# The fp16 remainder of the squared activation: VectorE or GpSimd

## Chip, cores and metric

The kernel runs on one core of a Trainium2 chip. The core has five engines with queues of their own: TensorE (PE in the profile, with PEld for its weight loads), VectorE (DVE), ScalarE (ACT), GpSimd (POOL) and SyncE (SP), which issues the DMAs here. Each engine takes its instructions in the program's order and waits for the others by semaphores. The metric is the device time of one execution in microseconds.

## What is computed

The reference is a block-causal attention over 8 batches, 8 heads, 576 positions and a head size of 64, whose output is the input of a two-layer network with a squared ReLU. Everything is fp32.

```python
scores = scale * np.matmul(q, k.transpose(0, 1, 3, 2))
scores = np.where(block_i >= block_j, scores, -1000000000.0)   # blocks of 64
attn = np.exp(scores - np.max(scores, axis=-1, keepdims=True))
attn = attn / (np.sum(attn, axis=-1, keepdims=True) + 1e-09)
attn_out = np.matmul(attn, v)
...
x = attn_out.transpose(0, 2, 1, 3).reshape(4608, 512)
h = x @ w_in            # 512 x 2048
r = np.maximum(h, 0.0)
g = r * r
return g @ w_out        # 2048 x 512
```

## The kernel before

TensorE multiplies fp16 faster than fp32, so each fp32 operand is split into an fp16 number and an fp16 remainder. A product of two such operands is the sum of three fp16 matmuls: high times high, high times remainder, remainder times high. The inputs, the probabilities (`p_rows`), the normalized attention output (`xt`), both weights (`w1h`, `w1l`, `w2h`, `w2l`) and `g` are all kept as such pairs.

The 4608 tokens are worked on in 12 chunks of 384 (`CH`), numbered `ck` 0 to 11; the hidden size of 2048 is 16 tiles of 128, numbered `f`. For each chunk, `moe_in` makes the 16 hidden tiles and `moe_out` the three output tiles:

- L670: 12 matmuls make `ph` (128 x 384) of one `f` in PSUM. There are two such banks (pool `ps_m`), which `po` of `moe_out` shares.
- L676: ScalarE writes `r` = relu(`ph`) to SBUF, in a ring of three buffers.
- L678: ScalarE writes `g[:, 0]`, the square of `r` rounded to fp16.
- L679: GpSimd writes `r*r` in fp32 over `r`.
- L680: `g[:, 1]` = `r*r` - `g[:, 0]`, the fp16 remainder. GpSimd does this for `f` below 8 (`G_POOL`) of chunk 0 (`G_CK` is 1), VectorE for the other 184 of the 192 tiles. The `r` buffer is free after it.
- L695: 48 matmuls make each output tile `po` from the 16 pairs `g`; for each `f` the remainder is read by the third matmul, after the two that read `g[:, 0]`.
- L702: VectorE scales `po` into `ob`, and a DMA writes it out.

The attention runs beside this. A pass covers one pair of heads of one batch: `scores` on TensorE (L411 for fp32 operands, L422 for fp16 pairs), maxima on VectorE (L446, L449), exp on ScalarE (L452), sums and reciprocals on VectorE (L460, L461), the pair `p_rows` on ScalarE (L475) and VectorE (L476), a transposing DMA into `p_turned` (L480), and the product with v on TensorE (L534), which ScalarE writes to `x` (L541). `front` prepares the next pass: maxima of the loaded `qk` and `v` (L363, L364), scales by way of TensorE (L177 to L191) and the fp16 pairs of q, k and v (L382 to L400). `load` brings the operands of the pass after that.

When the four head pairs of a batch are done for a group of rows, `normalize` works out their norms (L579 to L595), and GpSimd multiplies `x` by them (L604), VectorE rounds to fp16 (L605), and GpSimd makes the remainder (L606). A batch has two such groups, so there are 16. The result is what `moe_in` reads.

In the first 250 us the weights are split as well (`weight_scale`, `weight_parts`, L245 to L292), with integer work on VectorE and the remainders `w1l` and `w2l` on GpSimd (L292).

The order of all this comes from two places. `fill`, with the tables `FILL` and `DELAY`, lays the steps of the chunks between the passes as the program is written; then the framework's scheduler orders the instructions of each engine by its own model of their durations (`schedule_with_timeline_sim=TLS`). An engine that is given to an instruction can so change the order of others.

Of the kernel before, what the change touches and what calls it, by code (L numbers as in the profile page):

```python
# [14 lines left out]
ALU = mybir.AluOpType  # L15
# [26 lines left out]
SCN = 1  # L42
PTN = 3
PT0 = 16
G_POOL = 8
G_CK = 1
X_POOL = 1
QF = (6, 7)
WT = 1
# [51 lines left out]
def attention_moe_kernel(ctx: ExitStack, tc: tile.TileContext, qkt, qk, vm, vt, w_in, w_out, out):  # L101
    nc = tc.nc
# [524 lines left out]
    def moe(ck):  # L627
        gs = yield from moe_in(ck)
        yield from moe_out(ck, gs)

    def first_moe(ck, firsts):

        scale, parts = weight_scale(1), weight_parts(1)
        hidden = moe_in(ck)
        n = 0
        while True:
            try:
                next(hidden)
            except StopIteration as e:
                gs = e.value  # L640
                break
            if n == IVN:
                for r in firsts:
                    inverses(*r)
            yield
            if next(parts0, 0) is None:
                yield
            for _ in range(SCN if n >= SC0 else 0):
                if next(scale, 0) is None:
                    yield  # L650
            if n == PT0:
                yield from scale
            for _ in range(PTN if n >= PT0 else 0):
                if next(parts, 0) is None:
                    yield
            n += 1
        for gen in (scale, parts):
            yield from gen
        yield from moe_out(ck, gs)

    def moe_in(ck):
        xt = xts.pop(ck)
        gs = []
        c = 2.0 ** (1 - A_X - A_W)
        for f in range(NF):
            ph = ps_m.tile([P, 512], F32, tag="mm", name=f"ph_{ck}_{f}")
            i = 0
            for cc in range(NHP):
                for w, z in ((w1h, 0), (w1h, 1), (w1l, 0)):
                    nc.tensor.matmul(  # L670
                        ph[:, :CH], w[:, f, P * cc : P * cc + P], xt[:, z, cc, :], start=(i == 0), stop=(i == 11)
                    )
                    i += 1
            r = p2.tile([P, 512], F32, tag="r", name=f"r_{ck}_{f}", bufs=3)
            r = r[:, :CH]
            nc.scalar.activation(r, ph[:, :CH], AF.Relu, scale=c)  # L676
            g = pg.tile([P, 2, CH], F16, tag="g", name=f"g_{ck}_{f}")
            nc.scalar.activation(g[:, 0], r, AF.Square)  # L678
            nc.gpsimd.tensor_tensor(r, r, r, op=ALU.mult)  # L679
            (nc.gpsimd if f < G_POOL and ck < G_CK else nc.vector).tensor_tensor(g[:, 1], r, g[:, 0], op=ALU.subtract)  # L680
            gs.append(g)
            yield
        return gs
# [204 lines left out]
```

## Time and profile before

| what | value |
|---|---|
| three runs, us | 1150.38, 1157.13, 1152.78 |
| median, us | 1152.78 |
| the profiled execution's own time, us | 1157.18 |
| its span in the profile, us | 1155.4 |
| mean granted TensorE clock | 0.963 |
| instructions | 18711 |

The span runs from the first instruction of the profile to the last; 1.8 us lie around it. In the profile's rows `out<-in` names the tiles written and read, L680 is line 680 of the kernel, and an arrow `<-` behind a wait names the instruction that ended it. A matmul's duration is its time in the pipeline, so successive matmuls overlap.

### The profile page before, as it was taken

Reading aid. Unit: us, or ns where it says so; the run is one execution under the profiler, and the core shown is the slowest. Engines: PE = TensorE matmul, PEld = TensorE weight load, DVE = VectorE, ACT = ScalarE, POOL = GpSimd, SP = SyncE. Lnnn points to the kernel's source line nnn. Section 1 sums busy time; section 2 is a strip of 40 time slices with the busy share of each in tenths; the row PEclk is TensorE's granted clock in tenths of the full one; section 3 lists DMA queues with packets and bytes.
Section 4 is the critical chain, followed back from the end, with each engine's and each line's share of the span. In section 5 each row is a group of like instructions: output and inputs, shape, how many; then the busy total and the mean of one; then the engine's idle time right before and its main releaser. Section 6 shows DMA issues by size and latency. Waiting matters only on the chain. (4 is left out here: it accounts for less than half of the span.)

```text
span 1155.4 us, 18711 instructions
## 1 busy us (share of the span) xinstructions
PE 1035.3 (90%) x6836; PEld 541.6 (47%) x6836; DVE 763.9 (66%) x1783; ACT 629.6 (54%) x1492; POOL 341.0 (30%) x312
## 2 busy tenths in 40 slices
PE   6679777898989989899997999889889999999998
PEld 4234322354445445445544545445445545555453
DVE  6998789869778978868749857976896613212120
ACT  6586765557468548726737627726865723223140
POOL 2575145124112412422205302520340314312030
PEclk9799998899999999999999999989999999999999
DMA  8555177867687688855954657567848330000000
GB/s 282 194 186 194 56 193 188 198 140 140 144 165 156 114 191 164 155 115 114 186 120 84 141 111 138 119 140 148 170 80 169 48 78 20 10 19 1 28 1 28
DMA packets 337948, 142.25 MB, mean 123 GB/s; under 512 B 309696, under 2 KB 323008, under 8 KB 337856
## 3 DMA queue, kind: packets, MB, share of 16 engines
q1 hardware_dynamic: 337856, 141.06, 55.2%
q8 instruction: 53, 0.87, 0.3%
q14 instruction: 39, 0.32, 0.1%
HBM read 55.31 MB, written 9.44 MB: 56 GB/s over the span
## 5 line engine op out<-in xcount | busy, mean ns | idle before, releaser
L670 PE MATMUL ph<-xt,w1h 128*128 128x384 f16 x1536 | 381.2, 330 | 21.7 <-ACT r L676 10.4
L695 PE MATMUL po<-w2h,g 128*128 128x512 f16 x1152 | 359.7, 386 | 8.5 <-ACT w2h L291 8.5
L679 POOL TENSOR_TENSOR r<-r 128x384 f32<-128x384 f32 x192 | 178.6, 936 | 556.4 <-ACT g L678 520.3
L695 PEld LDWEIGHTS <-g 128*128 128x128 f16 x1728 | 166.3, 99 | 219.4 <-issue 34.1
L670 PE MATMUL ph<-xt,w1l 128*128 128x384 f16 x768 | 253.3, 330 | 0.0
L695 PE MATMUL po<-w2l,g 128*128 128x512 f16 x576 | 222.1, 386 | 4.2 <-POOL w2l L292 4.2
L670 PEld LDWEIGHTS <-w1h 128*128 128x128 f16 x1536 | 145.0, 99 | 129.6 <-issue 34.4
L452 ACT ACTIVATE p<-ps,nmx,es 128x320 f32<-128x320 f32 (+8 forms) x216 | 131.1, 616 | 135.9 <-DVE nmx L449 111.4
L676 ACT ACTIVATE r<-ph 128x384 f32<-128x384 f32 x192 | 93.2, 491 | 160.3 <-PE ph L670 147.9
L680 DVE TENSOR_TENSOR g<-r,g 128x384 f16<-128x384 f32 x184 | 113.7, 623 | 86.3 <-POOL r L679 86.2
L476 DVE SCALAR_TENSOR_TENSOR p_rows<-p,rs,p_rows 128x320 f16<-128x320 f32 (+8 forms) x240 | 143.5, 632 | 18.6 <-ACT p_rows L475 18.3
L475 ACT ACTIVATE p_rows<-p,rs 128x320 f16<-128x320 f32 (+8 forms) x240 | 120.3, 569 | 47.1 <-DVE rs L461 23.1
L446 DVE TENSOR_REDUCE nmx<-ps 128x1 f32<-128x192 f32 (+8 forms) x288 | 124.6, 479 | 23.5 <-PE ps L422 14.8
L678 ACT ACTIVATE g<-r 128x384 f16<-128x384 f32 x192 | 99.4, 525 | 4.0 <-POOL w1l L292 0.8
L670 PEld LDWEIGHTS <-w1l 128*128 128x128 f16 x768 | 75.8, 99 | 51.2 <-issue 2.2
L422 PE MATMUL ps<-kT,qT 128*64 128x64 f16 (+6 forms) x960 | 84.7, 297 | 10.6 <-DMA qT<-qs 5.8
L534 PE MATMUL px<-p_turned,v 128*64 128x384 f16 (+5 forms) x1168 | 79.3, 282 | 14.5 <-DMA p_turned<-p_rows 10.1
L702 DVE TENSOR_SCALAR ob<-po,uv 128x512 f32<-128x512 f32 x36 | 28.9, 805 | 95.7 <-PE po L695 95.7
L534 PEld LDWEIGHTS <-v 128*64 128x64 f16 x1128 | 54.7, 115 | 48.1 <-issue 22.1
L604 POOL TENSOR_TENSOR x<-x,hb 128x768 f32<-128x768 f32 (+1 forms) x16 | 44.6, 2785 | 94.9 <-DVE hb L595 92.8
L422 PEld LDWEIGHTS <-qT 128*64 128x64 f16 x960 | 45.9, 111 | 50.5 <-issue 31.7
L606 POOL TENSOR_TENSOR xt<-x,xt 128x768 f16<-128x768 f32 (+1 forms) x16 | 51.7, 3229 | 30.9 <-DVE xt L605 24.3
(129 smaller groups left out, 965.3 us busy)
## 6 DMA issues: line engine op xcount, KB each, us to landing
qk<-in_qk SPq DMA_DIRECT2D x24, 576.0 KB, 4.5
wa<-in_w_out SPq DMA_DIRECT2D x16, 512.0 KB, 4.3
wb<-in_w_out SPq DMA_DIRECT2D x16, 512.0 KB, 4.4
out<-ob SPq DMA_DIRECT2D x32, 256.0 KB, 2.1
vraw<-in_vm SPq DMA_DIRECT2D x30, 256.0 KB, 3.5
w1raw<-in_w_in SPq DMA_DIRECT2D x8, 512.0 KB, 6.6
kf<-in_qkt SPq DMA_DIRECT2D x8, 288.0 KB, 3.6
w2h<-in_w_in SPq DMA_DIRECT2D x4, 512.0 KB, 10.9
```

The costliest lines, as they stand in the source:

```text
L422: nc.tensor.matmul(ps[hs, o].rearrange("p (n d) -> p n d", d=D), t["qT"][:, j, hs], t["kT"][:, z, c0:c1, hs], start=(z == 0), stop=(z == 1),)
L446: nc.vector.tensor_reduce(nmx[:, i : i + 1], ps[:, off : off + w], axis=AX.X, op=ALU.max, negate=True)
L452: nc.scalar.activation(p32[:, off : off + w], ps[:, off : off + w], AF.Exp, bias=nmx[:, i : i + 1], scale=es, accum_out=sm[:, i : i + 1],)
L475: nc.scalar.activation(hi, p32[:, off : off + w], AF.Copy, scale=rs[:, i : i + 1])
L476: nc.vector.scalar_tensor_tensor(lo, p32[:, off : off + w], rs[:, i : i + 1], hi, op0=ALU.mult, op1=ALU.subtract)
L534: nc.tensor.matmul(px[hs, D * a :].rearrange("p (j d) -> p j d", d=D), lhs, rhs, start=(c == 0 and pi == 0), stop=(c == NCH[g] - 1 and (pi ...
L670: nc.tensor.matmul(ph[:, :CH], w[:, f, P * cc : P * cc + P], xt[:, z, cc, :], start=(i == 0), stop=(i == 11))
L676: nc.scalar.activation(r, ph[:, :CH], AF.Relu, scale=c)
L678: nc.scalar.activation(g[:, 0], r, AF.Square)
L679: nc.gpsimd.tensor_tensor(r, r, r, op=ALU.mult)
L680: (nc.gpsimd if f < G_POOL and ck < G_CK else nc.vector).tensor_tensor(g[:, 1], r, g[:, 0], op=ALU.subtract)
L695: nc.tensor.matmul(po, gs[f][:, z, P * t : P * t + P], w[:, f, :], start=(i == 0), stop=(i == 3 * NF - 1))
```

## The change

The subtraction of L680 is put on GpSimd for all tiles of all chunks, in the queue in which the product of L679 stands. The two constants that chose the engine go, and with them two lines, so that line 680 of before is line 678 of the changed kernel, L679 is L677, L604 is L602 and L606 is L604 there.

```diff
-G_POOL = 8
-G_CK = 1
...
             nc.scalar.activation(g[:, 0], r, AF.Square)
             nc.gpsimd.tensor_tensor(r, r, r, op=ALU.mult)
-            (nc.gpsimd if f < G_POOL and ck < G_CK else nc.vector).tensor_tensor(g[:, 1], r, g[:, 0], op=ALU.subtract)
+            nc.gpsimd.tensor_tensor(g[:, 1], r, g[:, 0], op=ALU.subtract)
```

No operation is added or dropped: 184 instructions change their engine, and the scheduler orders the rest anew. Two places show how.

GpSimd, before, at the end of the third chunk (`ck` 2), where the normalizing of batch 2 falls into it (the number after `r_` is `f`, then a buffer number; `hb_0` and `hb_1` are the norms of the two groups):

```order
L679 TENSOR_TENSOR r_11_3956<-r_11_3956 128x384
L679 TENSOR_TENSOR r_12_3975<-r_12_3975 128x384
L604 TENSOR_TENSOR x_88<-x_88,hb_0_4135 128x768
L679 TENSOR_TENSOR r_13_4023<-r_13_4023 128x384
L679 TENSOR_TENSOR r_14_4046<-r_14_4046 128x384
L679 TENSOR_TENSOR r_15_4065<-r_15_4065 128x384
L606 TENSOR_TENSOR xt_4127<-x_88,xt_4127 128x4x192
L604 TENSOR_TENSOR x_88<-x_88,hb_1_4152 128x1536
```

GpSimd, in the changed kernel, the same place:

```order
L677 TENSOR_TENSOR r_12_3975<-r_12_3975 128x384
L677 TENSOR_TENSOR r_13_4023<-r_13_4023 128x384
L602 TENSOR_TENSOR x_88<-x_88,hb_0_4135 128x768
L678 TENSOR_TENSOR g_12_3977<-r_12_3975,g_12_3977 128x384
L678 TENSOR_TENSOR g_13_4025<-r_13_4023,g_13_4025 128x384
L677 TENSOR_TENSOR r_14_4046<-r_14_4046 128x384
L604 TENSOR_TENSOR xt_4127<-x_88,xt_4127 128x4x192
L678 TENSOR_TENSOR g_14_4048<-r_14_4046,g_14_4048 128x384
L677 TENSOR_TENSOR r_15_4065<-r_15_4065 128x384
L678 TENSOR_TENSOR g_15_4067<-r_15_4065,g_15_4067 128x384
L602 TENSOR_TENSOR x_88<-x_88,hb_1_4152 128x1536
```

The subtractions of tiles 12 and 13 stand behind the multiplication of `x`, that of tile 14 behind the remainder of `x`, and that of tile 15 ahead of the next group's multiplication.

VectorE, before, around the norms of the same group:

```order
L592 TENSOR_SCALAR hb_0_4135<-nq_0_4129 128x192
L680 TENSOR_TENSOR g_11_3958<-r_11_3956,g_11_3958 128x384
L400 SCALAR_TENSOR_TENSOR v_3_1_0_3842<-vraw_81,s_1_0_3822,v_3_1_0_3842 128x640
L595 TENSOR_SCALAR hb_0_4135<-hb_0_4135 128x192
L680 TENSOR_TENSOR g_12_3977<-r_12_3975,g_12_3977 128x384
L446 TENSOR_REDUCE nmx_1_0_4_4073<-ps_1_0_4_4071 128x1 x3
L476 SCALAR_TENSOR_TENSOR p_rows<-p_3_0_0_8_3982,rs_0_0_8_3985,p_rows 128x576
```

VectorE, in the changed kernel, the same place:

```order
L590 TENSOR_SCALAR hb_0_4135<-nq_0_4129 128x192
L474 SCALAR_TENSOR_TENSOR p_rows<-p_3_0_0_7_3911,rs_0_0_7_3914,p_rows 128x512
L474 SCALAR_TENSOR_TENSOR p_rows<-p_3_0_0_7_3911,rs_0_0_7_3914,p_rows 128x384
L362 TENSOR_REDUCE st_3_0_4448<-vraw_81 128x1
L444 TENSOR_REDUCE nmx_1_0_7_4254<-ps_1_0_7_4252 128x1 x2
L474 SCALAR_TENSOR_TENSOR p_rows<-p_3_0_0_7_3911,rs_0_0_7_3914,p_rows 128x128
L444 TENSOR_REDUCE nmx_1_0_7_4254<-ps_1_0_7_4252 128x1
L447 TENSOR_SCALAR nmx_1_0_4_4073<-nmx_1_0_4_4073,es_1_0_3826 128x4
L593 TENSOR_SCALAR hb_0_4135<-hb_0_4135 128x192
L582 TENSOR_TENSOR sq_1_0_4144<-sq_1_0_4144 128x384
L474 SCALAR_TENSOR_TENSOR p_rows<-p_3_0_0_8_3982,rs_0_0_8_3985,p_rows 128x576
```

The two subtractions are gone from between the attention's instructions, and the second step of the norms (L595, now L593) stands eight places behind the first instead of three, with rows of `p_rows` and maxima between them.

## The prediction

> **What bounds the kernel now.** I read first the page's busy shares, then the stretches of the run one by one, then who waits for whom between 90 and 960 us, and last the chain of waits.
>
> ```profile
> PE 1035.3 (90%) x6836; PEld 541.6 (47%) x6836; DVE 763.9 (66%) x1783; ACT 629.6 (54%) x1492; POOL 341.0 (30%) x312
> ```
>
> TensorE (PE) is the bound, but not everywhere. The table of busy time by stretch shows where it is not; after the stretch and its length, the columns are PE, weight loads, VectorE (DVE), ScalarE (ACT) and GpSimd (POOL), then granted clock, DMA share and GB/s.
>
> ```profile
> 0.00:90.00 90.00, 60.50 (x418) 35.27 (x418) 76.30 (x200) 59.88 (x160) 47.86 (x65) 0.89 0.69 223
> 90.00:250.00 160.00, 130.40 (x746) 60.26 (x747) 128.66 (x292) 98.91 (x217) 56.98 (x52) 0.91 0.65 163
> 250.00:400.00 150.00, 136.70 (x992) 73.03 (x991) 122.36 (x282) 96.44 (x234) 41.16 (x31) 0.97 0.70 141
> 400.00:600.00 200.00, 183.45 (x1323) 97.11 (x1323) 145.05 (x359) 118.97 (x290) 45.49 (x37) 0.98 0.74 151
> 600.00:800.00 200.00, 183.11 (x1273) 95.59 (x1270) 150.98 (x341) 112.76 (x273) 57.75 (x41) 0.96 0.63 126
> 800.00:960.00 160.00, 150.25 (x1073) 80.11 (x1068) 101.48 (x241) 94.01 (x224) 44.71 (x37) 0.99 0.55 105
> 960.00:1155.00 195.00, 190.91 (x1030) 100.19 (x1028) 39.03 (x71) 48.64 (x96) 47.05 (x50) 1.00 0.04 14
> ```
>
> Three regimes stand in it. After 960 us attention is over and PE works 190.91 of 195 us: nothing another engine gains there counts. From 250 to 960 us PE is idle for 13.30 + 16.55 + 16.89 + 9.75 = 56.5 of 710 us, with VectorE at 63 to 82%. From 90 to 250 us PE is idle for 29.6 of 160 us, with VectorE at 80%. So at most 86.1 us can be gained by feeding PE better, and only a part of that hangs on VectorE. What PE and VectorE wait for between 90 and 960 us (total us, times, longest):
>
> ```profile
> PE px L534 <- DMA p_turned<-p_rows: 10.1, 7, 2.5
> PE ph L670 <- ACT r L676: 8.7, 12, 2.1
> PE nq L589 <- DVE sq L584: 8.0, 5, 2.8
> PE ph L670 <- DVE ob L702: 7.0, 5, 3.1
> DVE st L364 <- DMA vraw<-in_vt: 43.6, 16, 7.5
> DVE st L363 <- DMA qk<-in_qk: 21.3, 10, 4.6
> DVE g L680 <- POOL r L679: 19.4, 16, 3.8
> ACT r L676 <- DVE g L680: 12.3, 7, 3.7
> ```
>
> PE's waits are many and short; most lead to VectorE's attention work, directly (sq, ob) or through a transpose DMA that VectorE feeds. Two rows concern the moved instruction itself: VectorE stands 19.4 us at the head of its queue before a subtraction whose product GpSimd has not finished, and ScalarE waits 12.3 us for an r buffer that a late subtraction still reads.
>
> **What is removed.** The first four rows are durations (min/median/max in ns in the first two, total us and mean ns in the next two); the others are the subtraction's own time by stretch, in the columns of the table above.
>
> ```profile
> L680 DVE TENSOR_TENSOR g<-r,g x184: 523/550/3750, 99.0 to 1121.9; 128x384 f16<-128x384 f32 x184
> L680 POOL TENSOR_TENSOR g<-r,g x8: 912/1224/1425, 59.2 to 92.6; 128x384 f16<-128x384 f32 x8
> L680 DVE TENSOR_TENSOR g<-r,g 128x384 f16<-128x384 f32 x184 | 113.7, 623 | 86.3 <-POOL r L679 86.2
> L679 POOL TENSOR_TENSOR r<-r 128x384 f32<-128x384 f32 x192 | 178.6, 936 | 556.4 <-ACT g L678 520.3
> 90.00:250.00 160.00, 40.88 (x144) 13.96 (x144) 8.17 (x14) 6.92 (x14) 1.09 (x1) 0.91 0.65 163
> 960.00:1155.00 195.00, 97.23 (x448) 43.48 (x446) 27.37 (x48) 25.07 (x48) 0.00 (x0) 1.00 0.04 14
> ```
>
> VectorE loses 184 subtractions of 623 ns, 113.7 us. Of these 27.4 us lie after 960 us, behind PE, and are worth nothing; 8.2 us lie in 90 to 250; the other 78.1 us (122 of them) lie in 250 to 960, some 15% of VectorE's 520 us there. The 19.4 us at the head of its queue go too, though the next instruction may then wait for something else.
>
> **What is added.** GpSimd gets 184 subtractions. Its eight now take 912 ns at the least and 1224 at the median, nearly all in VectorE's busiest stretch. Taking 1.0 us, the minimum raised by about what the products show (936 mean), GpSimd goes from 341 to about 525 us, 45% of the span. That alone is covered: from 250 to 960 us it would work 189 + 122 of 710 us. After 960 us the pace is tightest:
>
> ```profile
> 1026.35 31.20 PE ph L670 x192
> 1057.55 31.08 PE po L695 x144
> L679 POOL TENSOR_TENSOR r<-r x192: 817/827/1844, 57.5 to 1121.0; 128x384 f32<-128x384 f32 x192
> ```
>
> PE makes a ph tile in 31.20/16 = 1.95 us; product and subtraction take 0.83 + 0.91 = 1.74 us on GpSimd, so it keeps up. If each needed 1224 + 827 ns it would fall behind by 0.1 us a tile, under 2 us a chunk, and the output product reads its last g only after 45 of 48 matmuls of its first tile, some 9.7 us (31.08 x 45/144) after it begins. I count the tail at nothing.
>
> **The lock, the cost of the move.** VectorE and GpSimd stop each other. Two places of the timeline (start, us, instruction):
>
> ```profile
> 741.29 3.44 POOL L604 TENSOR_TENSOR x<-x,hb 128x1536 f32<-128x1536 f32 x1 [1.36 <-DVE m L185]
> 741.32 3.44 DVE L191 TENSOR_SCALAR s<-m 128x3 int32<-128x3 int32 x1
> 258.50 3.81 POOL L679 TENSOR_TENSOR r<-r 128x384 f32<-128x384 f32 x3 [7.23 <-ACT g L678]
> 259.43 1.35 DVE L387 SCALAR_TENSOR_TENSOR qs<-qk,s,qs 128x576 f16<-128x576 f32 x1
> ```
>
> A three-element operation takes 3.44 us because a GpSimd multiply of 3.44 us began 0.03 us earlier; three products take 3.81 us where 3 x 0.827 = 2.48 us was due. So each new subtraction can hold VectorE back. Its price lies between nothing and its whole 0.91 us. The rows above show what such pairs lose on the mean today: a product on GpSimd 936 - 827 = 109 ns, a subtraction on VectorE 623 - 550 = 73 ns. I take 0.2 us for a new subtraction, near these and about their sum, because it follows a product and VectorE then meets two GpSimd instructions in a row. A third of the 0.62 us saved is so given back, and two thirds remain. The point where nothing remains is 78.1/122 = 0.64 us.
>
> By the Trainium skill (SBUF — State Buffer, "Who interferes with whom") a VectorE instruction that has two SBUF inputs, or runs in a two-port mode, and a GpSimd instruction that reads SBUF exclude each other for the whole instruction, whichever started first. The row of 3.44 us agrees. Taken to the letter for every subtraction this gives the third rival below.
>
> **On the path.** The chain of waits holds these pieces between 804.05 us, near its beginning, and 910.46 us, from where PE bounds it (start, us, what):
>
> ```profile
> 804.05 0.07 DVE g L680
> 808.57 0.46 DVE g L680
> 821.09 0.70 DVE g L680
> 839.77 0.48 DVE g L680
> 845.75 0.11 DVE g L680
> 901.95 0.47 DVE g L680
> 904.67 0.94 DVE g L680 x2
> 910.46 15.76 PE ph L670 x96
> ```
>
> The moved instruction is on the chain for 3.23 of 106.4 us. If the 660 us from 250 to 910 are alike, that is 6.2 x 3.23 = 20.0 us. Two thirds of it after the lock is 13 us. Other paths stand just behind (VectorE waits 64.9 us for loads, PE 10.1 us for the transposes), which takes some away; the 19.4 us at the head of the queue add some. I take 12 us. In 90 to 250 us the eight subtractions of the first chunk save 8 x 0.55 = 4.4 us, but in that dense stretch GpSimd's take 1224 ns rather than 912, so the lock bites both; I take nothing, with 4.4 us as the other end. What is late next is PE's own work and the loads.
>
> The sum is 1157.2 (the profiled execution's own time) - 12 = 1145.2 us. That execution is 0.4% above the median of the runs, 1152.78; in its measure the forecast is 1145.2 x 1152.78/1157.18 = **1141 us**.
>
> **The rivals.** *Nothing to see (about 1151 us).* The time freed on VectorE turns into longer waits for loads: the rows of 43.6 and 21.3 us show VectorE already waiting at the head of its queue, and a load that is issued no earlier returns no earlier. For it: PE is at 92 to 94% from 400 to 960 us. Against it: the chain runs through the subtraction at seven places. About 2 us gained. That the change might not do what it says is settled by the order: all 192 subtractions stand on GpSimd.
>
> *Slower (about 1162 us), by GpSimd's queue.* The subtractions now stand in one queue with the normalizing of x, which waits for the norms:
>
> ```profile
> POOL x L604 <- DVE hb L595: 85.0, 9, 36.9
> L604 POOL TENSOR_TENSOR x<-x,hb 128x768 f32<-128x768 f32 (+1 forms) x16 | 44.6, 2785 | 94.9 <-DVE hb L595 92.8
> L606 POOL TENSOR_TENSOR xt<-x,xt 128x768 f16<-128x768 f32 (+1 forms) x16 | 51.7, 3229 | 30.9 <-DVE xt L605 24.3
> ```
>
> Where two subtractions stand behind L604, as the order shows in the third chunk, they wait 2.8 us and what L604 itself waits. There are three r buffers and two PSUM banks; at 1.95 us a tile a subtraction may be some 6 us late before ScalarE's L676 and then PE stop. L604, L606 and two pairs of product and subtraction are 2.8 + 3.2 + 3.5 = 9.5 us, 3.5 us too many. If that happens in six of the sixteen groups it costs 21 us, and 21 - 12 = 9 us is lost. It decides against the move from four such places on (4 x 3.5 = 14 us). For it: 85.0 us of waiting at that place today. Against it: today's products queue there in the same way, and PE waited for L676 only 8.7 us.
>
> *Slower (about 1161 us), by the lock at its full price.* Every subtraction from 250 to 960 us stops VectorE for all its 0.91 us: 122 x 0.91 = 111 us of VectorE against 78 saved, 33 us more. On the chain 20.0 of the 78.1 us counted, a quarter, so 33 us cost 8 us. For it: the row of 3.44 us. Against it: VectorE also has reductions from PSUM and pauses, and today's pairs lose 0.07 to 0.11 us, not 0.9.
>
> **How the numbers follow.** Forecast 0.50, nothing 0.30, slower by the queue 0.12, slower by the lock 0.08; so faster by over 0.5% (about what a measurement of this kernel can tell from no change) 0.50, within it 0.30, slower 0.20. The low end is 20.0 us with no lock and 4.4 us of the early stretch: (1157.2 - 24.4) x 0.9962 = 1128. The high end is the slower rival, (1157.2 + 9) x 0.9962 = 1162; both ends are needed to leave out no more than 2 in 10.
>
> **What would show it.** Right: VectorE's busy time falls by 114 us less 20 to 40 us of stretched instructions; GpSimd's rises to 500 to 550; PE's idle time in 250 to 960 falls from 56 to about 45 us; L676's wait for the subtraction shrinks; the tail stays at 31.2 + 31.1 us a chunk. Wrong: the subtraction's mean on GpSimd stands near 1.2 us, L476 and L387 stretch by a fifth, or PE's ph tiles wait for L676, and L676 for GpSimd's g, for more than 20 us. The scheduler has also reordered neighbours on every engine; a gain or loss of a few us may come from that alone, and this argument cannot see it.

## The result, and the profile after

The changed kernel is **slower**: 1173.03 us median (1170.63 to 1177.36, 4 runs) against 1154.95 us (1150.38 to 1161.2, 4 runs) of the kernel before beside it on the same chip, a ratio of 1.0152 with a 95% interval of 1.0119 to 1.0185. The forecast was 1141 us with a range up to 1162; the time lies outside it. The profiled execution took 1170.63 us with a span of 1168.9 us.

The page's busy times of the changed kernel show that the change did what it says:

```profile
PE 1040.9 (89%) x6836; PEld 543.2 (46%) x6836; DVE 706.8 (60%) x1599; ACT 630.0 (54%) x1492; POOL 504.6 (43%) x496
```

VectorE lost its 184 subtractions, but its busy time fell by 57.1 us (763.9 to 706.8) where they had taken 113.7: the other 1599 instructions became 56.6 us longer. GpSimd rose by 164 us. The table by stretch (columns as in the prediction's) says where TensorE lost:

```profile
250.00:400.00 150.00, 136.12 (x999) 72.75 (x998) 118.28 (x263) 98.89 (x242) 67.76 (x60) 0.98 0.71 145
400.00:600.00 200.00, 181.28 (x1283) 95.48 (x1283) 145.32 (x324) 118.78 (x291) 79.86 (x70) 0.97 0.69 143
600.00:800.00 200.00, 183.02 (x1276) 95.26 (x1271) 134.54 (x292) 109.10 (x264) 84.23 (x72) 0.97 0.63 128
800.00:960.00 160.00, 146.25 (x1048) 78.91 (x1047) 97.75 (x221) 95.81 (x231) 68.24 (x68) 0.98 0.59 109
```

PE is idle for 13.88 + 18.72 + 16.98 + 13.75 = 63.3 us from 250 to 960 us, 6.8 us more than before, although VectorE is busy less in every one of these stretches but one. The start of each chunk's first L676 (L674 after) tells when: before at 54.8, 231.5, 329.5, 430.7, 521.2, 608.5, 697.4, 796.1, 892.4 and 965.8 us, after at 55.9, 236.3, 333.7, 434.7, 526.2, 618.3, 704.6, 807.1, 904.5 and 979.3. The lag grows at several places (between the first two chunks 3.8 us, between the fifth and sixth 4.7), is 13.5 us at the tenth chunk and stays so to the end: the tail did not change.

Who waited for whom between 90 and 960 us in the changed kernel (total us, times, longest):

```profile
PE px L532 <- DMA p_turned<-p_rows: 12.5, 9, 2.7
PE pm L181 <- DVE dg L180: 11.2, 7, 5.0
PE ph L668 <- ACT r L674: 10.0, 13, 2.1
DVE st L361 <- DMA qk<-in_qk: 34.5, 16, 6.9
ACT p L450 <- DVE nmx L447: 134.9, 40, 17.8
ACT r L674 <- POOL g L678: 3.5, 4, 1.2
```

The waits that the change was to shorten are short: ScalarE waits 3.5 us for an `r` buffer, not 12.3, and VectorE's 19.4 us before the subtraction are gone. PE waits a little longer in many places, no one of them new or large. The groups by line (busy us, mean ns) show what became longer; the last three rows are those of the kernel before for L458, L447 and L474, whose lines there are two higher:

```profile
L678 POOL TENSOR_TENSOR g<-r,g 128x384 f16<-128x384 f32 x192 | 189.8, 994 | 8.8
L458 DVE TENSOR_SCALAR sm<-sm 128x2 f32<-128x2 f32 (+2 forms) x104 | 30.3, 292 | 44.0 <-ACT p L450 43.9
L447 DVE TENSOR_SCALAR nmx<-nmx,es 128x4 f32<-128x4 f32 (+2 forms) x72 | 37.9, 526 | 0.6
L474 DVE SCALAR_TENSOR_TENSOR p_rows<-p,rs,p_rows 128x320 f16<-128x320 f32 (+8 forms) x240 | 158.8, 701 | 25.8 <-ACT p_rows L473 25.7
...
L460 DVE TENSOR_SCALAR sm<-sm 128x2 f32<-128x2 f32 (+2 forms) x104 | 27.2, 262 | 30.8 <-ACT p L452 30.2
L449 DVE TENSOR_SCALAR nmx<-nmx,es 128x4 f32<-128x4 f32 (+2 forms) x72 | 20.9, 290 | 0.3
L476 DVE SCALAR_TENSOR_TENSOR p_rows<-p,rs,p_rows 128x320 f16<-128x320 f32 (+8 forms) x240 | 143.5, 632 | 18.6 <-ACT p_rows L475 18.3
```

The subtraction takes 994 ns, as assumed. L447, which multiplies the two to four maxima of each row by a scale before softmax's exp, went from 290 to 526 ns on the mean. Four rows of the timeline (start, us, instruction), the shortest, median and longest time of L447 (ns), and two pieces of the chain of waits of the changed kernel show how:

```profile
853.14 0.95 DVE L447 TENSOR_SCALAR nmx<-nmx,es 128x4 f32<-128x4 f32 x1
853.17 1.78 POOL L678 TENSOR_TENSOR g<-r,g 128x384 f16<-128x384 f32 x2
915.96 1.78 POOL L678 TENSOR_TENSOR g<-r,g 128x384 f16<-128x384 f32 x2
916.00 0.89 DVE L447 TENSOR_SCALAR nmx<-nmx,es 128x3 f32<-128x3 f32 x1
L447 DVE TENSOR_SCALAR nmx<-nmx,es x72: 207/229/3395, 251.3 to 919.0; 128x4 f32<-128x4 f32 x24, 128x3 f32<-128x3 f32 x24, 128x2 f32<-128x2 f32 x24
853.23 0.87 DVE nmx L447
916.08 0.82 DVE nmx L447
```

Twice an operation whose median is 229 ns takes 0.95 and 0.89 us as two subtractions start on GpSimd within 0.04 us of it, and both times it stands on the chain, since exp on ScalarE waits for it.

So there were two suspects. **Theory A:** the scheduler's new order costs the time, and the move alone would have gained or done nothing. **Theory B:** the subtractions on GpSimd cost it, by the lock (B1), by GpSimd's queue ahead of L604 and L606 (B2), or because TensorE gets the remainder later (B3).

### The profile page after: what moved, and what is told of

Same layout as the page of the kernel before. It is cut to its first block, busy times and chain, and to the rows that moved or that the text cites. A ratio compares the mean times of both kernels' runs of the same rounds, so it can differ in the third digit from the quotient of the medians.

```text
span 1168.9 us, 18736 instructions
## 1 busy us (share of the span) xinstructions
PE 1040.9 (89%) x6836; PEld 543.2 (46%) x6836; DVE 706.8 (60%) x1599; ACT 630.0 (54%) x1492; POOL 504.6 (43%) x496
## 5 line engine op out<-in xcount | busy, mean ns | idle before, releaser
L677 POOL TENSOR_TENSOR r<-r 128x384 f32<-128x384 f32 x192 | 175.8, 920 | 417.2 <-ACT g L676 411.4
L678 POOL TENSOR_TENSOR g<-r,g 128x384 f16<-128x384 f32 x192 | 189.8, 994 | 8.8
L474 DVE SCALAR_TENSOR_TENSOR p_rows<-p,rs,p_rows 128x320 f16<-128x320 f32 (+8 forms) x240 | 158.8, 701 | 25.8 <-ACT p_rows L473 25.7
L674 ACT ACTIVATE r<-ph 128x384 f32<-128x384 f32 x192 | 93.0, 488 | 142.8 <-PE ph L668 109.4
L676 ACT ACTIVATE g<-r 128x384 f16<-128x384 f32 x192 | 99.4, 523 | 4.1 <-POOL w1l L290 0.9
L420 PE MATMUL ps<-kT,qT 128*64 128x64 f16 (+5 forms) x960 | 85.8, 294 | 12.9 <-ACT p L450 5.5
L602 POOL TENSOR_TENSOR x<-x,hb 128x768 f32<-128x768 f32 (+1 forms) x16 | 43.9, 2742 | 87.8 <-DVE hb L593 79.2
L532 PEld LDWEIGHTS <-v 128*64 128x64 f16 x1128 | 54.0, 112 | 45.4 <-issue 24.6
L458 DVE TENSOR_SCALAR sm<-sm 128x2 f32<-128x2 f32 (+2 forms) x104 | 30.3, 292 | 44.0 <-ACT p L450 43.9
```

The source lines that it names most:

```text
L420: nc.tensor.matmul(ps[hs, o].rearrange("p (n d) -> p n d", d=D), t["qT"][:, j, hs], t["kT"][:, z, c0:c1, hs], start=(z == 0), stop=(z == 1),)
L474: nc.vector.scalar_tensor_tensor(lo, p32[:, off : off + w], rs[:, i : i + 1], hi, op0=ALU.mult, op1=ALU.subtract)
L532: nc.tensor.matmul(px[hs, D * a :].rearrange("p (j d) -> p j d", d=D), lhs, rhs, start=(c == 0 and pi == 0), stop=(c == NCH[g] - 1 and (pi ...
L678: nc.gpsimd.tensor_tensor(g[:, 1], r, g[:, 0], op=ALU.subtract)
```

## The experiments

To hold the order still, most of these kernels fix the order of issue of every engine to the one of the kernel before ("old order") or of the changed kernel ("new order"), by dependencies that carry no wait; in the traces VectorE and ScalarE issue in the order so given. Line numbers are those of the kernel before. The core of the addition:

```diff
+            if last is not None:
+                tc.add_manual_dep(
+                    i, last.name,
+                    mybir.DependencyInfo(mybir.DependencyClass.NoSync, mybir.DependencyReason.DATA),
+                    reason="order of use",
+                )
+            last = i
```

Where a subtraction or a product is not on the engine that it has in the recorded order, the scheduler places it. Ratios are to the kernel before, run on the same chip.

### Order and engine apart

Old order, all subtractions on GpSimd:

```diff
-            (nc.gpsimd if f < G_POOL and ck < G_CK else nc.vector).tensor_tensor(g[:, 1], r, g[:, 0], op=ALU.subtract)
+            SUBS.append(nc.gpsimd.tensor_tensor(g[:, 1], r, g[:, 0], op=ALU.subtract))
```

> All subtractions on GpSimd as in the changed kernel, but every other instruction pinned to the order of issue that it had before; only the place of the subtractions in GpSimd's queue is free. If the loss comes from the scheduler's new order of the other instructions, this run is at the time of before or under it (1143 to 1157 us). If it comes from GpSimd holding VectorE back, or from GpSimd's queue, it stays at the changed kernel's 1170 to 1177 us.

Measured: 1154.12 us, ratio 0.9984 (0.9967 to 1.0000).

New order, the subtractions on VectorE as before (the line of L680 unchanged but for the list that names it):

> The reverse: the engines of before (184 subtractions on VectorE), every other instruction pinned to the order of issue of the changed kernel. If the new order costs the time, 1170 us or more, since VectorE also has its 114 us again. If the lock or GpSimd's queue costs it, about 1155 us as before.

Measured: 1168.03 us, ratio 1.0116 (1.0079 to 1.0153), 2 us under what was expected of the order. The order alone makes the kernel slower; the engine alone does nearly nothing.

No subtraction at all, old order (the third matmul of `po` reads the rounded square):

```diff
-            (nc.gpsimd if f < G_POOL and ck < G_CK else nc.vector).tensor_tensor(g[:, 1], r, g[:, 0], op=ALU.subtract)
...
-                for z, w in ((0, w2h), (0, w2l), (1, w2h)):
+                for z, w in ((0, w2h), (0, w2l), (0, w2h)):
```

> The subtraction is left out on both engines (the third matmul of the output reads the rounded square again, the same work for TensorE), order of before. It shows what taking the subtraction off VectorE is worth when GpSimd gets nothing for it. My prediction's path term says 20 us or a little more: 1130 to 1138 us. If the subtractions on VectorE were hidden anyway, 1150 us or more.

Measured: 1132.54 us, ratio 0.9799 (0.9772 to 0.9826): what the subtractions cost on VectorE is 2.0%, some 23 us. The same in the new order:

> Leaves out the subtraction (the third matmul of po reads the rounded square again), in the changed kernel's order of instructions. If the order and the subtraction add up, this is 2% below the run with the subtractions on VectorE in the same order (ratio 1.0116): a ratio of 0.990 to 0.995, 1146 to 1151 us. If the new order costs time only because of where it puts the subtractions, there is nothing left of that cost here: 0.980, 1133 us.

Measured: 1145.12 us, ratio 0.9898 (0.9860 to 0.9935), at the lower edge of what adding up gives. Together:

| ratio to before | subtractions on VectorE | on GpSimd | none |
|---|---|---|---|
| old order | 1 | 0.9984 | 0.9799 |
| new order | 1.0116 | 1.0152 | 0.9898 |
| cost of the new order | 1.2% | 1.7% | 1.0% |

Theory A stands: the new order costs 1.0 to 1.7% in each column, even where there is no subtraction to place. The cells 1 and 1.0152 are the two kernels themselves, which were not run with their own order fixed; the last column is fixed in both rows and shows the cost without them. But the first row shows a second thing: 2.0% was to be had and 0.16% came.

A part of these differences goes with the granted TensorE clock. In the runs of the kernel before, whose median clock is 0.966, a clock lower by 0.01 goes with some 6 us more. By this estimate the clock stands for 1 to 2 us of the loss in the first two columns (medians in the new order 0.964 and 0.963), and for some 4 of the 13 us between the two kernels without a subtraction (0.973 and 0.9655). Whether the order lowers the clock was not tested.

### Where the order loses it

GpSimd subtracts everywhere; the new order holds in one third of the program and the old one in the rest, cut at TensorE's matmuls 1600 and 3900 of 6604.

> All subtractions on GpSimd; the changed kernel's order up to TensorE's matmul 1600 of 6604 (about 330 us), the order of before from there. The whole new order costs 17 to 19 us over 1154. One bad place in this third: 1170 and the other two at 1154. Spread over the kernel as the starts of the chunks say (5 of 17.7 us lost by there): 1159.

> The same with the changed kernel's order between TensorE's matmuls 1600 and 3900 alone (about 330 to 690 us). By the starts of the chunks 3 of 17.7 us are lost there: 1157. One bad place: 1170 here or 1154.

> The same with the changed kernel's order from matmul 3900 (about 690 us) to the end. By the starts of the chunks 10 of 17.7 us are lost there: 1164. One bad place: 1170 here or 1154.

Measured: 1.0001 (0.9983 to 1.0019), 1.0010 (0.9989 to 1.0031) and 1.0044 (1.0023 to 1.0065), against 0.9984 with the old order throughout. There is no single bad place: the thirds cost 0.2, 0.3 and 0.6%. They add up to 1.0%, not the 1.7% of the whole; with intervals of 0.2 to 0.4% on each of these ratios it is open whether that difference is real. Which reordered instructions do the harm was not found.

### What gives the gain back in the old order

If GpSimd's queue is to blame (B2), it must be by the subtractions that stand shortly ahead of its work on `x`. Only those 60 on GpSimd, the other 132 left out, and then the reverse (left out as above: the third matmul of `po` reads the rounded square). The table gives the first and last `f` in each chunk; the first three of chunk 5 belong to the 60 too:

```diff
+NEAR = {1: (10, 14), 2: (9, 15), 3: (8, 15), 4: (12, 15), 5: (10, 13), 6: (3, 13), 7: (8, 15), 8: (10, 15), 9: (11, 14)}
```

> Order of before. Only the 60 subtractions that stand shortly ahead of GpSimd's products L604 and L606 run, on GpSimd; the other 132 are left out (there the third matmul of po reads the rounded square again). Against 1132.5 us with no subtraction and 1154 with all of them on GpSimd: if the loss is the shared lock, it goes by their number, 60 of some 160 ahead of the tail, +8 us, 1140. If it is GpSimd's queue ahead of L604 and L606, nearly all of it is here: 1150 to 1154.

> The complement: the 132 subtractions that do not stand ahead of L604 and L606 run on GpSimd, the other 60 are left out. Lock: 100 of some 160 ahead of the tail, +13 us on 1132.5, 1145. Queue: 1133 to 1136.

Measured: 1142.44 us, 0.9873 (0.9839 to 0.9906), and 1144.88 us, 0.9898 (0.9873 to 0.9922). Above 0.9799 that is 0.74% for 60 and 0.99% for 132: by number rather than by place (0.12% for ten of the first, 0.10% for ten of the 100 of the second that lie in the chunks 0 to 9), and the two add up to 1.73%, close to the 1.85% of all. In this order B2 falls.

Subtractions on GpSimd that nobody reads, old order (they are all made, and the third matmul of `po` reads the rounded square):

> Order of before, all subtractions on GpSimd, but nothing reads what they write: the third matmul of po takes the rounded square again, which leaves the remainder out of the result. Lock or GpSimd's time: as with all subtractions on GpSimd in this order, 1150 to 1156. If the gain is given back because TensorE gets the remainder later from GpSimd (0.99 us and its queue) than from VectorE (0.57 us): as without any subtraction, 1131 to 1137.

Measured: 1154.47 us, 0.9978 (0.9960 to 0.9996), the same as when they are read. B3 falls.

For the lock, a write in place of the subtraction: it occupies GpSimd about as long (958 ns on the mean), but reads nothing. The third matmul of `po` again reads the rounded square.

```diff
+            rt, r = r, r[:, :CH]
...
+            SUBS.append(nc.gpsimd.memset(rt.bitcast(F16), 0.0))
```

In the new order first:

> Order of the changed kernel; in place of each subtraction GpSimd writes zeros over the r buffer, 1024 fp16 a partition, about 0.9 us in the same place of the same queue, reading nothing from SBUF (the remainder is left out, as in the run without subtractions). If the lock on reads costs the time, 1135 to 1155 us. If the new order or the length of GpSimd's queue costs it, about 1170 us.

Measured: 1159.84 us, ratio 1.0023 (0.9988 to 1.0058), between none (0.9898) and the subtractions (1.0152), and between the two expectations. Then in the old order:

> In place of each subtraction GpSimd writes 1024 fp16 zeros to r, about 0.9 us, so that the remainder is left out of the result (the third matmul of po takes the rounded square again); order of before. GpSimd is as busy as with the subtractions (495 of 505 us), but VectorE's instructions were stretched by half as much under such writes in the changed kernel's order (busy 664.5 without, 685.4 with the writes, 706.8 with the subtractions). If the time goes by VectorE's stretch, as in the five kernels of this order without a subtraction on VectorE (661 us busy and 1132.5 us to 708 and 1154.5, 0.47 us for each), this is at 680 to 685 busy and 1141 to 1145. If it goes by how long GpSimd is occupied: 1152 to 1156.

Measured: 1147.52 us, ratio 0.9916 (0.9896 to 0.9935), again between the two, and outside both expectations, for VectorE was stretched more than foreseen. The pages' busy times, in the order: no subtraction, write only, subtractions on GpSimd:

```profile
PE 1024.4 (90%) x6836; PEld 538.1 (48%) x6836; DVE 661.2 (58%) x1599; ACT 627.1 (55%) x1492; POOL 319.4 (28%) x304
PE 1035.9 (90%) x6836; PEld 543.1 (47%) x6836; DVE 696.1 (61%) x1599; ACT 628.5 (55%) x1492; POOL 495.4 (43%) x496
PE 1031.9 (90%) x6836; PEld 540.4 (47%) x6836; DVE 706.6 (61%) x1599; ACT 630.1 (55%) x1492; POOL 506.5 (44%) x496
```

And the groups of three of VectorE's lines in the same three kernels, same order:

```profile
L476 DVE SCALAR_TENSOR_TENSOR p_rows<-p,rs,p_rows 128x320 f16<-128x320 f32 (+8 forms) x240 | 141.3, 628 | 22.2 <-ACT p_rows L475 21.7
L460 DVE TENSOR_SCALAR sm<-sm 128x2 f32<-128x2 f32 (+2 forms) x104 | 30.3, 291 | 50.2 <-ACT p L452 49.7
L449 DVE TENSOR_SCALAR nmx<-nmx,es 128x4 f32<-128x4 f32 (+2 forms) x72 | 24.9, 345 | 0.6
...
L476 DVE SCALAR_TENSOR_TENSOR p_rows<-p,rs,p_rows 128x320 f16<-128x320 f32 (+8 forms) x240 | 139.2, 625 | 21.0 <-ACT p_rows L475 20.9
L460 DVE TENSOR_SCALAR sm<-sm 128x2 f32<-128x2 f32 (+2 forms) x104 | 40.3, 388 | 45.6 <-ACT p L452 45.5
L449 DVE TENSOR_SCALAR nmx<-nmx,es 128x4 f32<-128x4 f32 (+2 forms) x72 | 36.0, 515 | 0.6
...
L476 DVE SCALAR_TENSOR_TENSOR p_rows<-p,rs,p_rows 128x320 f16<-128x320 f32 (+8 forms) x240 | 150.6, 667 | 21.4 <-ACT p_rows L475 21.1
L460 DVE TENSOR_SCALAR sm<-sm 128x2 f32<-128x2 f32 (+2 forms) x104 | 35.6, 342 | 43.5 <-ACT p L452 43.4
L449 DVE TENSOR_SCALAR nmx<-nmx,es 128x4 f32<-128x4 f32 (+2 forms) x72 | 28.8, 400 | 0.6
```

GpSimd's subtractions make the same 1599 instructions of VectorE 45.4 us longer, 0.24 us for each subtraction; ScalarE's busy time hardly moves (627.1 to 630.1). With writes alone GpSimd is as busy, but L476, which reads two SBUF operands, keeps its 628 ns, VectorE is stretched by 34.9 us, and the cost is 1.17% instead of 1.85%. So GpSimd's being occupied does not explain the loss by itself, and B1 is what remains for at least the difference. In the old order, with no subtraction on VectorE and ScalarE's work as it was, the time goes up with VectorE's busy time from kernel to kernel: 661.2 us busy and ratio 0.9799, 677.9 and 0.9873 (60 subtractions), 689.5 and 0.9898 (132), 696.1 and 0.9916 (writes), 706.6 and 0.9984, 708.2 and 0.9978 (unread). That is 21 us for 45, about 0.47 us for each. GpSimd's busy time goes up along with VectorE's in these kernels (319.4, 384.8, 444.5, 495.4, 506.5 and 507.1 us), so their sequence alone does not name the cause; the writes are the one point that parts the two.

Where the stretch costs its time is not found. ScalarE's wait for L449 ahead of exp (90 to 960 us) is, in the old order, with no subtraction, with writes and with subtractions on GpSimd; in the kernel before; and in the new order with the subtractions on VectorE and with none:

```profile
ACT p L452 <- DVE nmx L449: 112.0, 31, 15.7
ACT p L452 <- DVE nmx L449: 101.1, 28, 15.5
ACT p L452 <- DVE nmx L449: 118.1, 34, 15.3
...
ACT p L452 <- DVE nmx L449: 117.0, 37, 15.9
...
ACT p L452 <- DVE nmx L449: 137.8, 40, 16.3
ACT p L452 <- DVE nmx L449: 140.1, 45, 16.1
```

It is shortest under the writes, where L449 takes longest, and with GpSimd's subtractions it is as before. It grows with the new order, also where GpSimd has no subtraction (with the writes from 101.1 to 114.5 us). So its growth to 134.9 us in the changed kernel goes with the order rather than with the longer L447.

### Taking GpSimd's other operation away

If each operation on GpSimd costs so much, the product can leave it. ScalarE makes it, old order, subtractions on GpSimd:

```diff
-            nc.gpsimd.tensor_tensor(r, r, r, op=ALU.mult)
+            nc.scalar.activation(r, r, AF.Square)
```

> Order of before, same result: the product r*r is made by ScalarE (activation Square) and GpSimd makes only the subtraction, so that GpSimd has again one operation for each row of a chunk. ScalarE gets 192 operations more. If GpSimd's second operation (by lock or by queue) is what gives the gain back, this comes out between 1132 and 1140 us, faster than both kernels, unless ScalarE, with 630 us busy, becomes late in attention, where softmax's exponentials stand on the path: then 1155 to 1175.

Measured: 1141.54 us, ratio 0.9878 (0.9835 to 0.9922): faster than both kernels, by 1.2% against before, and 1.5 us above the first expectation. VectorE is busy 674.3 us. The same with the subtractions on VectorE:

> Order of before, r*r on ScalarE, the subtraction on VectorE as before: GpSimd has no part of the activation. Lock: GpSimd's product is as long as its subtraction and blocks VectorE alike, so leaving it out wins what leaving the subtraction out of GpSimd won (12.6 us with ScalarE's added work): ratio 0.987 to 0.991, 1143 to 1147, and VectorE's busy time falls by about 40 us from 764. If what GpSimd's subtraction costs is particular to it (its place behind the product, not the lock), nothing is won and ScalarE's added work shows: 1155 to 1166, VectorE's busy time unchanged.

Measured: 1159.70 us, ratio 1.0028 (1.0009 to 1.0047). VectorE's busy time fell, as the lock says, by 35.7 us:

```profile
PE 1036.2 (89%) x6836; PEld 542.2 (47%) x6836; DVE 728.2 (63%) x1783; ACT 713.7 (62%) x1684; POOL 163.7 (14%) x120
DVE g L680 <- ACT r L679: 59.1, 45, 4.7
```

but the second row, a wait of VectorE between 90 and 960 us, is 39.7 us more than the 19.4 that it waited for GpSimd's product before: ScalarE makes the square later, and VectorE stands at the head of its queue for it. One ate the other, so this run tells nothing about the lock's price in time.

Last, the same text as the 1141.54 us kernel with the order left to the scheduler:

> The changed kernel with r*r made by ScalarE (activation Square) in place of GpSimd, in the order that the scheduler itself gives to this text; the same work on each engine as in the run of 1141.5 us with the order of before. If the order is worth 1 to 1.7%, either way, this lies anywhere from 1141 to 1160; if the order mattered only through GpSimd's two operations in a row, 1139 to 1144.

Measured: 1180.60 us, ratio 1.0210 (1.0178 to 1.0242), outside the expectation.

```profile
PE 1037.8 (88%) x6836; PEld 545.1 (46%) x6836; DVE 677.6 (57%) x1599; ACT 711.5 (60%) x1684; POOL 340.0 (29%) x304
```

The engines do the same work (VectorE 677.6 us against 674.3, ScalarE 711.5, GpSimd 340.0) in another order, and it takes 39 us more, 3.4%. The median granted clock is lower too, 0.9555 against 0.9715, which by the estimate above stands for some 9 of the 39 us. The cost of the order does not come with GpSimd's two operations in a row.

## Why the prediction was wrong

- **What failed first: "a gain or loss of a few us may come from that alone, and this argument cannot see it".** The scheduler's reordering was named and then given no size, no chance and no place in the range. It costs 13 us with the subtractions on VectorE and 19 us with them on GpSimd (1.2 and 1.7%), more than the whole forecast gain, and it gives the result its sign. The order views had shown that neighbours moved on every engine; a rival with a price was missing.
- **What failed second: "A third of the 0.62 us saved is so given back".** The stretch was too small in the sum, and so was its weight. On the mean of all 192 subtractions it is 0.24 us, but nearly all of it falls on the 144 ahead of the tenth chunk: in the old order VectorE is busy 696.45 us up to there with them on GpSimd and 651.18 with none, which is 0.31 us for each against the 0.2 taken; by the text's own working that gives back half, and 10 us remain. The text then priced VectorE's lost time like its gained time, at a quarter of a microsecond for each. Measured ahead of the tenth chunk, where VectorE is busy 726.46 us before and 651.18 without the subtraction, a microsecond of subtraction is worth 23 us in 75, 0.31, but a microsecond of stretch costs 0.47. Nine tenths of the gain were given back (21 of 23 us). Why the stretch costs more is open: the two pieces of L447 on the chain suggest softmax's instructions, but ScalarE's wait for L449 did not grow with the stretch. Nor do the runs price the lock alone: the writes occupy GpSimd as long, and their cost of 1.17% may hold a share of that.
- **The path term was right.** 20.0 us from the chain of waits; 23 us measured without the subtractions (20 to 26), some 4 of which go with a higher granted clock (0.973 against 0.966).
- **The rival by the lock** had the right side, 1161 us, by luck: with the old order the move is not slower, and its price was 0.91 us for each subtraction. Break-even was all but reached at 0.31 us, not at 0.64. By the Trainium skill (SBUF — State Buffer, "Who interferes with whom") a VectorE instruction with two SBUF inputs collides with a GpSimd instruction that reads SBUF but not with one that only writes, while tensor_scalar may take a two-port mode and collide with either. The runs agree for L476, which stays at 625 ns under the writes, and for L449, which goes from 345 to 515; L400 and L387, also with two SBUF operands, grew by 6 and 5%.
- **The rival by GpSimd's queue** is refuted: the 60 subtractions ahead of L604 and L606 cost no more than their share asks, to within the intervals of the two runs, and PE waited 10.0 us for L674, 8.7 before.
- **"Nothing" in the tail and in the early stretch** held for the move itself: the chunks of the tail start 62.4 us apart (31.2 + 31.1), and with the old order the second chunk starts at 230.8 us, before at 231.5. The 236.3 us of the changed kernel is the order's. In the tail ScalarE waits 29.8 us for `r` buffers (28.9 until an L677 and 0.9 until an L678 ends), but PE waits for none of it.
- **Of the signs named to tell right from wrong,** VectorE's busy time (57 us less, not 74 to 94) and PE's idle time (63, not 45) came out wrong; GpSimd's busy time (504.6 us) and the wait for the `r` buffer (3.5 us) came out right. None of those named for "wrong" came: the subtraction took 994 ns, L474 stretched by 11% and L385 (L387 before) by 4%, not by a fifth. They watched GpSimd and the mean stretch, and not the order.

## What to carry to other kernels

Where a scheduler orders the instructions, an edit is two changes, and the second can be the larger: fix the old order, move only what the edit moves, and compare; here one and the same text ran in 1141.5 and 1180.6 us. Time freed on an engine and time lost on it can have different prices (0.31 and 0.47 here): measure both, the first by leaving the operation out. Before giving GpSimd a second operation beside a busy VectorE, look whether another engine can take the first.

## What was not expected of the hardware

A GpSimd write that reads nothing (L680 as a memset of 1024 fp16, 958 ns on the mean) still stretched VectorE's scalar operations on two to four numbers a row. In the old order it did so more than the subtraction did: L449 515 ns against 400, L460 388 against 342, 345 and 291 without either. In the new order L449 took 533 ns against 526 in the changed kernel and 347 without either, so for L449 the difference between the two is not settled. L476, with two SBUF operands, it left alone (625 ns against 628); L400 and L387 grew (926 ns against 873, 1024 against 979), less than under the subtraction (960 and 1103).
